# First z of a fused attention and expert kernel loaded in two parts, z copies issued by GpSimd, routing labels summed in two steps, last products reordered

## Chip, cores and metric

One Trainium2 chip, one core of it. The time is the device time of one execution in microseconds, lower is better. The engines are named as in the profile: PE (TensorE, products), PEld (its weight loads), DVE (VectorE), ACT (ScalarE), POOL (GpSimd), SP (SyncE, which here only issues DMAs). All data are float32 unless said otherwise.

## What is computed

Two blocks, one after the other: a gated attention unit over 8 batches of 2496 tokens, and a mixture of 8 experts to which each token goes by a hash of its id.

```python
batch, seq, d_model, d_qk = 8, 2496, 256, 64
def _attn_ref(u, v, z):
    scale = 1.0 / S
    scores = scale * np.matmul(z, z.transpose(0, 2, 1))
    attn = np.maximum(scores, 0.0) ** 2
    out = np.matmul(attn, v)
    return (u * out).astype(np.float32)

def _moe_ref(x, token_ids, w1, w2):          # x: (19968, 256), w1: (8, 256, 1024), w2: (8, 1024, 256)
    expert_idx = token_ids * np.int64(2654435761) % np.int64(8)
    for e in range(8):
        mask = expert_idx == e
        h = np.maximum(x[mask] @ w1[e], 0.0)
        out[mask] = h @ w2[e]
```

## The kernel before

**Attention.** A batch is cut into 5 groups of queries and 5 tiles of keys, so 25 steps, 200 in all; `pos` is the place of a step in its group (0 to 4). A step multiplies squared scores with v into an accumulator in PSUM (`attend`, L330), by a scheme with seven products for a 2x2 block product; the sums that it needs are made by DVE (`sums`, L279 to L282, and `add_v`, L218 to L221). Scores are symmetric: they are computed (`score`, L255 on PE, relu and square on ACT, L259 to L268, one square on DVE, L264) for key tiles not before the group, and else recalled from a mirrored copy in DRAM that earlier steps transposed (L295) and stored (L303, L307, on SP's queue). At `pos` 4 `join` (L341 to L349) adds the accumulators up, and the next group can only write a bank when `join` has read it. Scores are made two steps ahead (`AHEAD = 2`).

**z.** The scores need z transposed, `zT`, with the 64 values of a key on partitions 0 to 63 and the same again on partitions 64 to 127, for the second half of the keys. A batch has 78 blocks of 32 tokens, loaded in four pieces, `ZB = ((0, 16), (39, 55), (16, 39), (55, 78))`. `load_z` (L164) issues the loads of a piece, `turn_z` (L177) transposes it on DVE (L190, L192), up to 8 blocks an instruction. For batch 0, `twice(b)` holds: z is loaded to both halves of the partitions, so a piece has four loads instead of two, and at once before the first step. For each later batch, in the batch before, piece c is loaded at step 5 + 4c of it, turned at step 10 + 4c, and `copy_z` (L195) sends the lower half of the partitions to the upper by a DMA at step 11 + 4c; the fourth copy thus stands at step 23 of 25, and the scores of the next batch that read it are made from step 25 on. The z pool has two buffers, so the third piece waits for the first to be turned.

**Order.** The order of the work is written out by hand: each engine and each DMA queue takes its instructions in the order of the program. In one step that order is: sums and scores two steps ahead, storing mirrors, loading, turning and copying z of the next batch, `attend`, `join`, one mirror, loads of v, gating, one piece of the routing, sorting, up to two scatters of token numbers. SP's queue carries the stores of mirrors, the loads of z, the copies of zT, and the fetches (`x_row`, L376) and `u` loads (L227) for gating. POOL issues the scatters of gated rows (`sort`, L415, which wait for DVE), of token numbers (`enter`, L700), of zeros (L691), and the loads and stores of prepared weights (L722, L746).

**Routing.** `places` is a generator that computes from the token ids where each token goes. One piece of it, up to the next `yield`, is run at each step that is in `ROUTE`: not at `pos` 4, not in the first group of a batch. The piece with the labels (L542 to L545) falls on step 13, at `pos` 3, just ahead of a join.

**Experts.** Tokens of one expert stand in blocks of 512. In iteration `i` of the last loop, `up_big` of block i (seven products for each half of the hidden width, 14 parts, `U`), `down_big` or `down_last` of block i - 1 (seven parts, `D`) and `turn_x` of block i + 1 (`X`) are interleaved by a string of letters, `ORDER`; a letter runs its generator to the next `yield`. A lower case letter is the one small block.

**Start.** PE first multiplies an identity with itself (`warm`, L827), while z arrives.

## Time and profile before

| | us |
|---|---|
| three runs | 2425.05, 2430.60, 2436.82; median 2430.6 |
| the profiled execution | 2431.11 |
| its span, from first to last instruction | 2429.3 |
| PE busy in it | 2412.5 |
| attention, until the last scores are made | about 1426 |
| mean granted PE clock | 0.998 of full speed |

A line of the timeline gives start in us, length in us, engine, source line, operation, what is written and read, shapes, and how many instructions are merged; in square brackets, how long the engine had been idle and what ended that. An f32 product is two passes on PE, so a step's numbers of products stand doubled. The list of waits gives total us, times and the longest. A windows line gives start and end, length, then busy us and count of PE, PEld, DVE, ACT and POOL, then the granted PE clock, the share of the DMA engines' time and GB/s. A DMA's row is the issue of it; the landing is told apart.

### The profile page before, as it was taken

The page shows a single profiled execution, that of the slowest core. Times are in us where ns is not written, and L with a number is a line of the kernel's source. Part 1 is how long each engine was busy: PE and PEld are TensorE (multiplying, and loading weights), DVE is VectorE, ACT ScalarE, POOL GpSimd, SP SyncE. Part 2 cuts the span into 40 slices and gives each one's busy share as a digit, 9 for nine tenths or more (in the row PEclk, how much of TensorE's full clock was granted, in tenths as well). Part 3 has the DMA queues.
Part 4 walks back from the last instruction along what each step waited for, and adds up shares of the span by engine and source line. Part 5 has one row for each costly group of instructions (what it writes and reads, how often), then busy time and mean ns, then how long its engine had stood idle before and what let it go on. Part 6 is the DMA issues. An engine that isn't in the chain of part 4 may idle for free.

```text
span 2429.3 us, 32806 instructions
## 1 busy us (share of the span) xinstructions
PE 2412.5 (99%) x11247; PEld 2015.3 (83%) x11247; DVE 1817.1 (75%) x3808; ACT 725.7 (30%) x1210; POOL 694.6 (29%) x741
## 2 busy tenths in 40 slices
PE   9999999999999999999999999999999999999998
PEld 7787787787787787787787788989898988888887
DVE  7778788868868868868868667777777777777774
ACT  4324314314324314314324212222222222222221
POOL 0000101433433433433423112232323323232323
PEclk9999999999999999999999999999999999999999
DMA  7874667788788888788887776868777776867682
GB/s 152 219 197 111 161 181 217 230 278 254 238 261 252 229 269 253 229 277 245 247 241 226 210 228 213 267 219 261 239 234 259 230 256 217 259 223 252 226 270 101
DMA packets 423642, 554.61 MB, mean 228 GB/s; under 512 B 256129, under 2 KB 350161, under 8 KB 405041
## 3 DMA queue, kind: packets, MB, share of 16 engines
q1 hardware_dynamic: 350704, 327.02, 48.1%
q0 software_dynamic: 40320, 127.63, 15.0%
q10 hardware_dynamic: 32448, 97.86, 12.1%
q8 instruction: 88, 1.44, 0.2%
q14 instruction: 82, 0.66, 0.1%
HBM read 352.23 MB, written 196.06 MB: 226 GB/s over the span
## 4 chain that ended last, share of the span: by engine, by line
PE 97%; DMA 1%; DVE 1%; issue 1%; ACT 0%; POOL 0%; ACTq 0%; POOLq 0%; DVEq 0%
PE acc L330 49%; PE h_ps L1034 20%; PE o_ps L1072 19%; PE s_ps L255 9%; PE o_ps L1107 1%; DMA zT<-zT 1%; DMA a<-scores 0%; ACT a L259 0%; DMA zn<-in_z_dram 0%; POOL out_dram L976 0%; PE h_ps L1131 0%; DVE t L279 0%; DVE labels L543 0%; DVE t L281 0%; DVE t L280 0%
## 5 line engine op out<-in xcount | busy, mean ns | idle before, releaser
L259 ACT ACTIVATE a<-s_ps 128x512 f32<-128x512 f32 (+1 forms) x480 | 246.4, 600 | 728.3 <-PE s_ps L255 699.9
L330 PE MATMUL acc<-t,vc 128*128 128x256 f32 (+3 forms) x1600 | 402.3, 374 | 0.3 <-DVE t L279 0.3
L330 PEld LDWEIGHTS acc<-a,v_sb 128*128 128x128 f32 (+1 forms) x1600 | 295.2, 191 | 121.6 <-issue 46.5
L330 PE MATMUL acc<-a,v_sb 128*128 128x256 f32 (+3 forms) x1600 | 385.5, 384 | 1.1 <-DVE o L343 1.0
L415 POOL DMA_INDIRECT x_slots<-x_row,row x160 | 189.5, 1184 | 640.0 <-DVE x_row L393 534.2
L330 PE MATMUL acc<-t,v_sb 128*128 128x256 f32 (+3 forms) x1600 | 369.7, 373 | 0.0
L330 PEld LDWEIGHTS acc<-t,vc 128*128 128x128 f32 (+1 forms) x1600 | 303.3, 190 | 34.4 <-DVE t L279 0.7
L330 PEld LDWEIGHTS acc<-t,v_sb 128*128 128x128 f32 (+1 forms) x1600 | 303.4, 190 | 33.7
L1034 PE MATMUL h_ps<-xs,w 128*128 128x256 f32 (+1 forms) x1280 | 311.9, 376 | 0.0
L279 DVE TENSOR_TENSOR t<-a 128x512 f32<-128x512 f32 (+1 forms) x200 | 134.3, 672 | 209.1 <-ACT a L268 152.9
L1072 PE MATMUL o_ps<-h,w 128*128 128x256 f32 (+1 forms) x1216 | 283.9, 376 | 0.0
L1041 ACT ACTIVATE h<-h 128x512 f32<-128x512 f32 (+1 forms) x240 | 149.9, 625 | 410.6 <-DVE h L994 173.8
L1034 PEld LDWEIGHTS h_ps<-xs,w 128*128 128x128 f32 x1280 | 242.6, 190 | 28.7
L1072 PEld LDWEIGHTS o_ps<-h,w 128*128 128x128 f32 x1216 | 236.1, 195 | 23.7
L255 PE MATMUL s_ps<-zT 64*128 64x512 f32 (+1 forms) x960 | 240.9, 614 | 4.4 <-DMA zT<-zT 4.0
L1034 PE MATMUL h_ps<-xT,w 128*128 128x256 f32 (+1 forms) x960 | 231.1, 376 | 0.0
L295 DVE STREAM_TRANSPOSE mirror<-a 128x256 f32<-128x256 f32 x640 | 217.7, 406 | 0.0
L1072 PE MATMUL o_ps<-hs,w 128*128 128x256 f32 (+1 forms) x912 | 213.0, 376 | 0.6 <-DVE hs L1023 0.6
L976 POOL DMA_INDIRECT out_dram<-o_sb,idx x152 | 156.9, 1032 | 181.4 <-DMA o_sb<-o 146.7
L700 POOL DMA_INDIRECT slot_tokens<-token,addr x160 | 170.2, 1064 | 121.9 <-DVE addr L688 73.1
L330 PE MATMUL acc<-a,vc 128*128 128x256 f32 (+3 forms) x800 | 201.1, 373 | 0.0
L1034 PEld LDWEIGHTS h_ps<-xT,w 128*128 128x128 f32 x960 | 182.0, 190 | 22.2 <-DVE h L994 0.4
(193 smaller groups left out, 2634.5 us busy)
## 6 DMA issues: line engine op xcount, KB each, us to landing
w<-w_blocks SPq DMA_DIRECT2D x80, 1792.0 KB, 12.1
scores<-mirror SPq DMA_DIRECT2D x192, 256.0 KB, 4.8
a<-scores ACTq DMA_DIRECT2D x48, 1024.0 KB, 5.5
scores<-mirror SPq DMA_DIRECT2D x224, 128.0 KB, 3.1
a<-scores ACTq DMA_DIRECT2D x32, 896.0 KB, 5.5
w_blocks<-w POOLq DMA_DIRECT2D x16, 1792.0 KB, 8.8
u_sb<-in_u_dram SPq DMA_DIRECT2D x72, 256.0 KB, 4.9
xq<-x_slots SPq DMA_DIRECT2D x144, 128.0 KB, 12.6
```

What stands on the lines that cost most here:

```text
L255: nc.tensor.matmul(flat(ps)[:, 0:2 * w].rearrange("p (q c) -> p q c", q=2), tile_of_keys(b, h, s, j), q_h, start=True, stop=True)
L259: nc.scalar.activation(of[:, :, j, h].rearrange("p m q e -> p q m e"), flat(ps)[:, 0:2 * w].rearrange("p (q m e) -> p q m e", q=2, e=in_bl ...
L279: nc.vector.tensor_sub(t1, y12, y11)
L295: nc.vector.transpose(to, in_blocks(a, g)[:, :, j, h].rearrange("p i q (r t) -> p t i q r", t=2)[:, t])
L330: nc.tensor.matmul(acc[k][:, half, 0:w], x[0:n, j, :], y[0:n, j], start=(first and j == 0 and half == 0), stop=(last and j == 1), skip_gro ...
L415: st = nc.gpsimd.indirect_dma_start(out=x_dram[:, :], out_offset=bass.IndirectOffsetOnAxis(ap=row[0:m, c:c + 1], axis=0), in_=x_sb[0:m, q, ...
L700: st = nc.gpsimd.indirect_dma_start(out=slot_dram[:, None], out_offset=bass.IndirectOffsetOnAxis(ap=addr[0:n, to:to + 1], axis=0), in_=tok ...
L976: st = nc.gpsimd.indirect_dma_start(out=out[:], out_offset=bass.IndirectOffsetOnAxis(ap=idx[0:n, col:col + 1], axis=0), in_=o[0:n], in_off ...
L1034: nc.tensor.matmul(ps[:, r], w1[j][:, k, ts(f + r, P)], y, start=first and r == 0, stop=True, skip_group_check=True)
L1041: lambda o, i, k, ps=None: nc.scalar.activation(o, o if ps is None else ps, AF.Relu))
L1072: nc.tensor.matmul(ps, w2_block(w2[j], k)[:, f], x[:, f], start=first and f == 0, stop=f == FQ - 1, skip_group_check=True)
L1107: nc.tensor.matmul(ps[:, ts(t, P)], x[:, f, ts(t, P)], w2_block(w2[j], k)[:, f], start=first and t == 0 and f == 0, stop=f == FQ - 1, skip ...
```

## The change

Five edits.

1. The first two pieces of batch 0 (`ZB[0]` and `ZB[1]`, 16 blocks each) are loaded and turned in two parts of 8 blocks: first part of piece 0, first part of piece 1, turn both, then the second parts. So there are 16 loads instead of 8, alternating on SP's and ACT's queues as before, and the load of the first v tile is issued behind all of them, where it stood before the third piece's loads and still does.
2. The warm products are 9 instead of 12.
3. `copy_z` is issued by GpSimd instead of SP: 28 copies, 4 for each of batches 1 to 7. Their places in the program are as before, so on POOL each stands ahead of the scatters of its own step.
4. The labels (a reduction over 8 experts of 160 columns) are summed in two halves of 80 columns, with a `yield` between; the two instructions after it (`eid`) go with the second half. A `yield` inside a loop over two kinds of blocks, further on, is moved behind the loop, so two pieces become one. What lies between, masks, counting products, scan and rank sums, therefore runs one piece later; what comes after, as before.
5. The last iteration that has an `up_big` gets its own string: its last three letters are `UUD` instead of `UDU`, so the last down product of block NL - 2 stands behind the last up product.

```diff
@@ -103,6 +103,8 @@
     assert sorted(x for a, b in ZB for x in range(a, b)) == list(range(S // L))
     NZ = len(ZB)
 
+    FIRST = 8
+
     def pool(name, bufs, **kw):
         return ctx.enter_context(tc.tile_pool(name=name, bufs=bufs, **kw))
 
@@ -161,26 +163,27 @@
     uf, vf, zf = (x.rearrange("b s d -> (b s) d") for x in (u, v, z))
     zn, zT, v_sb, vc_sb, u_sb = {}, {}, {}, {}, {}
 
-    def load_z(b, c, engines=None):
-
-        j0, j1 = ZB[c]
+    def load_z(b, c, engines=None, at=slice(0, None)):
+
+        if not at.start:
+            zn[b, c] = zpool.tile([P, 24, L], F32, name="zn")
+        j0, j1 = range(*ZB[c])[at][0], range(*ZB[c])[at][-1] + 1
         n = j1 - j0
-        zn[b, c] = zpool.tile([P, 24, L], F32, name="zn")
         for i in range((P if twice(b) else K) // L):
             (nc.sync if engines is None else engines[i % len(engines)]).dma_start(
-                out=zn[b, c][ts(i, L), 0:n, :],
+                out=zn[b, c][ts(i, L), ds(at.start, n), :],
                 in_=zf[ds(b * S + j0 * L, n * L), ts(i % (K // L), L)].rearrange("(j r) k -> r j k", r=L))
 
     def twice(b):
         return b == 0
 
-    def turn_z(b, c):
-        j0, j1 = ZB[c]
-        if c == 0:
+    def turn_z(b, c, part=slice(0, None)):
+        j0 = ZB[c][0]
+        if c == 0 and not part.start:
             zT[b] = zpool.tile([P, S + L], F32, name="zT")
             nc.vector.memset(zT[b][:, S:S + L], 0.0)
         n = P if twice(b) else K
-        j = j0
+        j, j1 = range(*ZB[c])[part][0], range(*ZB[c])[part][-1] + 1
         while j < j1:
             g, first = divmod(j % (HS // L), 2 * QB)
             m = blocks(g)
@@ -194,7 +197,7 @@
 
     def copy_z(b, c):
         at = ds(ZB[c][0] * L, (ZB[c][1] - ZB[c][0]) * L)
-        nc.sync.dma_start(out=zT[b][K:P, at], in_=zT[b][0:K, at])
+        nc.gpsimd.dma_start(out=zT[b][K:P, at], in_=zT[b][0:K, at])
 
     def load_v(b, s, engine=None):
         engine = nc.sync if engine is None else engine
@@ -540,7 +543,10 @@
             nc.vector.tensor_tensor(mask[:], mask[:], label[:].unsqueeze(2).to_broadcast([P, E, C]), op=OP.mult)
             yield
             labels = route.tile([P, C], F32)
-            nc.vector.tensor_reduce(labels[:], mask[:].rearrange("p e c -> p c e"), axis=AX.X, op=OP.add)
+            for c in (slice(0, C // 2), slice(C // 2, C)):
+                nc.vector.tensor_reduce(labels[:, c], mask[:, :, c].rearrange("p e c -> p c e"), axis=AX.X, op=OP.add)
+                if not c.start:
+                    yield
             nc.vector.tensor_scalar(eid[:], eid[:], float(E), float(E), op0=OP.is_ge, op1=OP.mult)
             nc.vector.tensor_add(eid[:], eid[:], labels[:])
             yield
@@ -651,7 +657,7 @@
                 over = some[:, 0:nb * E].rearrange('p (j e) -> p j e', e=E)
                 nc.vector.tensor_tensor(over, *a_b(iota_b[:, 0:nb], end[0:1, :]), op=OP.is_ge)
                 nc.vector.tensor_reduce(of_block[:, b0:b0 + nb], over, axis=AX.X, op=OP.add)
-                yield
+            yield
             nc.vector.tensor_scalar(of_block[:], of_block[:], float(E - 1), None, op0=OP.min)
             over = some[:, 0:NB * E].rearrange('p (j e) -> p j e', e=E)
             nc.vector.tensor_tensor(over, *a_b(of_block[:], iota_e[0:1, :]), op=OP.is_equal)
@@ -823,15 +829,17 @@
 
 
     warm = mm_ps.tile([P, P], F32, name="warm", tag="mm")
-    for _ in range(12):
+    for _ in range(9):
         nc.tensor.matmul(warm[:], ident[:], ident[:], start=True, stop=True)
 
-    for c in range(NZ):
-        load_z(0, c, (nc.sync, nc.scalar) if c < 2 else None)
-        if c < 2:
-            turn_z(0, c)
-        if c == 1:
-            load_v(0, 0)
+    for part in (slice(0, FIRST), slice(FIRST, None)):
+        for c in range(2):
+            load_z(0, c, (nc.sync, nc.scalar), part)
+        for c in range(2):
+            turn_z(0, c, part)
+    load_v(0, 0)
+    for c in range(2, NZ):
+        load_z(0, c)
     for k in range(1, NT):
         load_v(0, k)
     AHEAD = 2
@@ -1151,7 +1159,8 @@
 
 
     ORDER = {"first": "UUUUGUUUGUUUUUUU", "second": "DUDUDUUDUUDUU" "XUxUDUXUDUUUU",
-             "other": "UuUDUuUXDUdUDU" "UDUDUxUDUXUDU", "end": "DDDDDDDd"}
+             "other": "UuUDUuUXDUdUDU" "UDUDUxUDUXUDU",
+             "last": "UuUDUuUXDUdUDU" "UDUDUxUDUXUUD", "end": "DDDDDDDd"}
 
 
     BIG, SMALL = [x for e in range(E) for x in (*range(e * FULL // E, (e + 1) * FULL // E), NL - 1 - e)], [[]] * (NL - 1) + [list(range(NL, NL + SMALLS))]
@@ -1173,7 +1182,7 @@
         if i == 0:
             x_sb = late.tile([P, 2, 2, D], F32, name="x_row")
             parts["G"] = gate_at_once(*done, x_sb, lambda: down_ps.tile([P, 2, D], F32, name="g_ps", tag="held", bufs=2))
-        for p in ORDER["first" if i == 0 else "second" if i == 1 else "end" if i == NL else "other"]:
+        for p in ORDER["first" if i == 0 else "second" if i == 1 else "end" if i == NL else "last" if i == NL - 1 else "other"]:
             next(parts.get(p, iter(())), None)
         for p in parts.values():
             assert next(p, None) is None and next(p, "end") == "end"
```

## The prediction

> **What bounds the kernel now.** I read the page's busy times first, then the list of what TensorE (PE) waited for, then the timeline around each of those waits, then the granted clock there. All lines here are of the kernel before.

> ```profile
> span 2429.3 us, 32806 instructions
> ...
> PE 2412.5 (99%) x11247; PEld 2015.3 (83%) x11247; DVE 1817.1 (75%) x3808; ACT 725.7 (30%) x1210; POOL 694.6 (29%) x741
> ```
> PE has no large hole: 16.8 us of the span without a product. An edit off PE can win only where PE waits or runs slowly. The waits (total us, times, longest):

> ```profile
> PE s_ps L255 <- DMA zT<-zT: 4.0, 2, 2.1
> ...
> PE acc L330 <- DVE o L343: 1.0, 1, 1.0
> ```
> The copies of zT that this change moves, and the join that the labels delay, head this short list. The first costs more than its 4.0 us. PE at the start of batch 4, then the same stretch of batch 6, which had no wait:

> ```profile
> 731.66 1.13 PE L255 MATMUL s_ps<-zT 64*128 64x512 f32 x2
> 734.72 2.27 PE L255 MATMUL s_ps<-zT 64*128 64x512 f32 x6 [1.93 <-DMA zT<-zT]
> 736.92 3.33 PE L330 MATMUL acc<-a,v_sb 128*128 128x256 f32 x8
> ...
> 744.50 0.71 PE L255 MATMUL s_ps<-zT 64*128 64x512 f32 x2
> ```
> ```profile
> 1099.83 2.00 PE L255 MATMUL s_ps<-zT 64*128 64x512 f32 x8
> 1101.75 1.99 PE L330 MATMUL acc<-a,v_sb 128*128 128x256 f32 x8
> ...
> 1107.99 2.00 PE L255 MATMUL s_ps<-zT 64*128 64x512 f32 x8
> ```
> From score to score batch 4 takes 744.50 - 731.66 = 12.84 us, batch 6 takes 1107.99 - 1099.83 = 8.16. So the stall cost 4.7, of which 1.93 is waiting. The rest is the eight products after it, 3.33 against 1.99, and their neighbours, and the clock column says why (the number before the DMA share and GB/s):

> ```profile
> 724.00:736.00 12.00, 10.07 (x45) 6.97 (x44) 10.54 (x25) 5.04 (x9) 0.00 (x0) 1.00 0.72 196
> 736.00:748.00 12.00, 12.00 (x45) 8.33 (x44) 10.30 (x28) 5.85 (x10) 7.18 (x7) 0.86 0.75 208
> ```
> 0.86 over 12 us is 3.4 us at half clock: an idle of 1.9 us was followed by slow products. Batch 5 has the same pair (score starts 915.67 and 928.66: 12.99, so 4.8 lost; clock 0.86 behind it). Together 9.5 us. The 1.0 us wait at the join was not followed by a lower clock (1.00).

> Why the copy was late in batch 4:

> ```profile
> 722.73 0.36 DVE L192 STREAM_TRANSPOSE zT<-zn 64x224 f32<-64x224 f32 x1
> ...
> 726.29 0.67 SPq L376 DMA_DIRECT2D x_row<-x  x1
> 727.05 0.96 SPq L227 DMA_DIRECT2D u_sb<-in_u_dram  x2
> 728.11 0.47 SPq L197 DMA_DIRECT2D zT<-zT  x1
> ```
> z was turned at 723.09. SP issued its copy at 728.11, behind a fetch (512 KB) and two u loads (256 KB each) that it had just sent on the same queue; it landed at about 734.6, 6.5 us later. The 28 copies land 2.2/3.4/6.8 us after issue (least, median, most).

> **The change, part by part.**

> *Copies on GpSimd.* The same 28 copies now follow POOL's order, not SP's. SP loses 28 issues of 0.48 us and the wait in front of each; nothing on PE's path waits for those issues but the copies themselves. On POOL the fourth copy of a batch stands ahead of the last scatter of token slots (L700) of the step before; what stands before it there ended before z was turned, in batches 3 to 7 (batch 4: 720.1 against 723.09; batch 5: 903.7 against 908.17). So it starts when z is turned, not 2.4 to 5.0 us after. From turned to the score that needs it there are 9.6, 8.6, 7.5, 9.3 and 11.1 us in batches 3 to 7; from SP's issue there were 6.9, 3.6, 3.6, 5.9 and 8.7. Batches 4 and 5 were those with 3.6. The trace has no such copy on POOL. Its issue is bounded by POOL's plain DMAs, 0.60 us (L746) and 0.87 us (L722); its landing from below by the fastest copy of SP, 2.2, from above by L746's 11.9 us for ten times the bytes. Nearest is SP's own copy: 3.4 median, and 2.2 to 4.5 where no 512 KB fetch is just ahead on its queue. I take 0.8 + 3.4 = 4.2 us, 3 us inside the tightest case, and 0.8 + 6.8 = 7.6 would miss batch 5 by 0.1. Both stalls and their slow clock go: -9.5 us. If all landings were as slow as L746's median of 8.8, batches 4 and 5 would stall by 0.2 and 1.3 us and about 1.5 would remain; -9.5 to 0 are the ends.

> What the copies delay on POOL: the eight scatters of zeros (L691), at 260.62 now, stand behind the second copy of batch 2, turned at 307.41; they take 28 us, so end near 336, and the scatter after them starts at 361.57 now. Then two L700 (361.57 to 364.9) stand before batch 2's fourth copy, which starts at 365.2 instead of 357.99: 7.8 us before 372.97, enough. An L700 at 1222.50 waits until 1242.60; the sort behind it runs at 1256.43 and the table is read at 1307. Each other delay is one issue. PE waits for none of these before the last stage.

> [...]

> *First z in parts.* PE's first score waits for both z blocks, whole:

> ```profile
> 0.74 1.99 SPq L170 DMA_DIRECT2D zn<-in_z_dram  x4
> 1.42 5.01 PE L827 MATMUL warm<-ident 128*128 128x128 f32 x24 [1.42 <-POOL ident masks.py:199]
> 6.33 0.77 DVE L190 STREAM_TRANSPOSE zT<-zn 128x256 f32<-128x256 f32 x2 [0.75 <-DMA zn<-in_z_dram]
> 6.83 4.41 PE L255 MATMUL s_ps<-zT 64*128 64x512 f32 x16 [0.40 <-DVE zT L190]
> ```
> Eight loads of 64 KB become sixteen of 32 KB; half the bytes come first. An issue costs 0.5 us at any of these sizes, so the last load of the first half is still the fourth on its queue, issued at 2.3. It lands no sooner than the first load did, 2.5 us after issue (4.8), and no later than now (6.3). With half the packets before it I take 5.2; a transpose of 0.42 and PE starts at 5.7 instead of 6.83: -1.1 us, ends 0 and -1.4 (nine warm products, 18 passes at 0.21, occupy PE until about 5.4). Behind it: the second half is issued by 4.9 and lands near 7.2, when PE has done the first score (5.7 + 1.9); ScalarE issues eight loads instead of four (until 4.9) and then loads its table (1.28), ready at 6.2 for a score at 6.9; v_sb is issued 1.3 us later and lands near 9.2 against 10.1 wanted; the third z block waits for its buffer until about 6.8 instead of 5.61, lands near 14.3 and is turned at about 14.2 to 16. All are covered, with 0 to 0.9 us to spare.

> The clock rose during the 24 warm passes: 0.21 us each at first, 0.11 at the end, the change at about 5.8, after 4.4 us of products. With nine, PE is busy up to that moment but for some 0.3 us. If the clock came 3.4 us later, scores at half speed would take back up to 1.7. [...]

> *Labels in two steps.* The join's first sum should have run before PE wanted the bank:

> ```profile
> 119.57 2.34 DVE L543 TENSOR_REDUCE labels<-mask 128x160 f32<-128x1280 bf16 x1
> ...
> 127.34 1.99 PE L330 MATMUL acc<-a,v_sb 128*128 128x256 f32 x8 [1.01 <-DVE o L343]
> ```
> Half the reduction (1.17 of 2.34) and L544, L545 (0.5 with their gaps) leave this step: DVE is free 1.7 us sooner, but the next square (L264) waits for ScalarE until 121.3 rather than running at 122.34. So the join moves by 1.0: -1.0 us, just the wait. All routing pieces up to the block table then run one step later: second half and L544/545 (1.7) where the mask (1.45) stood; the mask where DVE idled 1.66 soon after; the six count products and their ScalarE copies one step on; the scan (2.78) one set of sums later; the rank sum (1.49) before a wait of 0.42, with 3.17 idle next. Two loop pieces now share a step, so the rest of the routing stands where it did. If this cover were gone, the largest, the scan, would cost up to 2.8.

> *Last stage.* One down product (2 us on PE) changes place with the last up product. What can be won is the slow product at 2405.57: 2.06 against 1.95 to 1.98, so -0.1. The 0.58 wait behind it, for L988, remains. Two stores move 1 us later on an idle POOL.

> **Sum.** The profiled execution took 2431.1 us (span 2429.3 and 1.8 around it), 0.5 above the median of 2430.6. 2431.1 - 9.5 - 1.1 - 1.0 - 0.1 = **2419.4**, 0.46% below the median. About 0.5%, 12 us, is what a measurement of this kernel can tell from no change; the line is at 2418.4.

> **Rivals.** (A) The copies stay late: POOL's queue replaces SP's, and at least half of the 9.5 remains. For it: landings of 6.5 us in a stage whose DMA engines are 72 to 83% busy. Against it: starts 5.0 and 3.9 us earlier. Time: 2424 to 2429, say 2427; chance 0.15. (B) More is won: runs with a third stall, batch 6 having had only 5.9 us, make the median before dearer, and SP's queue, 28 waits shorter, brings loads sooner. A third stall is 4.7 more: 2415 against a like median; chance 0.2. (C) Slower: copies on POOL land over 11.1 us after z is turned, as only L746's slowest did (11.9). Then batches 3 to 7 all stall: 5 x 4.75 - 9.5 = +14.3 and, with the other gains of 2.2, 2443. It decides from a landing of about 10 us on; chance 0.05. (D) The split does nothing, because the second half's packets mix with the first's: 2420.5, within the forecast.

> **Chances.** The forecast (2416 to 2424, D included) 0.6. Faster by over 0.5%: B's 0.2 and 0.17 of the forecast's 0.6, 0.37. Slower: C, 0.05. Within: 0.58. Range for 8 in 10: 2413 to 2428, which holds the forecast and most of A and B.

> **What would show it.** Right: PE has no wait for zT, and no clock under 1.00 between the start and the end; the third score of batches 4 and 5 takes 8.16 us to the next; the first score starts near 5.7; no wait on L343's join. Wrong: a POOL copy that starts over 2 us after its transposes, or lands over 7 us after; a half clock in the first 12 us; a new wait of PE between 140 and 200 us.

## The result, and the profile after

The changed kernel takes 2422.01 us, median of 20 runs (2420.97 to 2423.88); the kernel before, 20 runs beside it, 2426.38 (2422.63 to 2436.82). The ratio is 0.9978, 95% interval 0.9972 to 0.9984: 4.4 us less at the medians, 0.2%, which is inside the 0.5% that the forecast called no change. The 2419.4 forecast is 2.6 us too low. The most telling figure is the spread: 14 us before, 3 us after.

The profiled executions are 2431.1 before and 2421.5 after, so this pair shows 9.6 us, twice the difference of the medians. The page of the changed kernel, its first lines:

```profile
span 2419.8 us, 32825 instructions
...
PE 2406.5 (99%) x11241; PEld 2011.5 (83%) x11241; DVE 1817.9 (75%) x3809; ACT 725.8 (30%) x1210; POOL 715.5 (30%) x769
```

What TensorE (PE) waited for in the changed kernel (total us, times, longest):

```profile
PE warm L833 <- POOL ident masks.py:199: 1.4, 1, 1.4
PE h_ps L1042 <- DVE h L1002: 0.9, 1, 0.9
PE s_ps L258 <- DVE zT L193: 0.8, 1, 0.8
PE o_ps L1080 <- DVE hs L1031: 0.6, 1, 0.6
```
The 4.0 us for copies of zT and the 1.0 us for the join are gone. The wait for zT that is left is for a transpose, at the very start, and it has grown from 0.4 to 0.8. The 0.9 for L1002 was not there before.

The third score of batch 4 and what follows, in PE's timeline after (start, duration, instruction), and the windows around it (length, busy time and count of PE, PEld, DVE, ACT and POOL, granted clock, DMA share, GB/s):

```profile
730.41 2.00 PE L258 MATMUL s_ps<-zT 64*128 64x512 f32 x8
732.34 1.99 PE L333 MATMUL acc<-a,v_sb 128*128 128x256 f32 x8
...
738.58 2.00 PE L258 MATMUL s_ps<-zT 64*128 64x512 f32 x8
```
```profile
732.00:744.00 12.00, 12.00 (x54) 9.06 (x53) 11.90 (x33) 7.73 (x12) 5.03 (x5) 1.00 0.62 154
```
738.58 - 730.41 = 8.17 instead of 12.84, and full clock. Batch 5 is the same (12.99 before, 8.17 after): 4.67 + 4.82 = 9.49 us, the forecast's 9.5. The copy, in POOL's timeline:

```profile
721.04 0.57 POOL L200 DMA_DIRECT2D zT<-zT  x1 [2.15 <-DVE zT L195]
```
z was turned at 720.7; the copy starts 0.3 us later, where SP's had started 5.0 later.

The start, in the timelines of VectorE and PE after:

```profile
3.71 0.45 DVE L193 STREAM_TRANSPOSE zT<-zn 128x256 f32<-128x256 f32 x1 [2.80 <-DMA zn<-in_z_dram]
4.71 0.45 DVE L193 STREAM_TRANSPOSE zT<-zn 128x256 f32<-128x256 f32 x1 [0.55 <-DMA zn<-in_z_dram]
5.95 0.45 DVE L193 STREAM_TRANSPOSE zT<-zn 128x256 f32<-128x256 f32 x1 [0.80 <-DMA zn<-in_z_dram]
```
```profile
1.43 4.21 PE L833 MATMUL warm<-ident 128*128 128x128 f32 x18 [1.43 <-POOL ident masks.py:199]
6.45 4.41 PE L258 MATMUL s_ps<-zT 64*128 64x512 f32 x16 [0.82 <-DVE zT L193]
```
Both first parts are turned at 5.16, where the forecast put the second at 5.6 (5.2 + 0.42). But the first score starts at 6.45, not 5.7: just when the third transpose ends (5.95 + 0.45). It is of the second part, columns that the first score does not read.

The labels in VectorE's timeline, and the join in PE's:

```profile
118.48 1.23 DVE L547 TENSOR_REDUCE labels<-mask 128x80 f32<-128x640 bf16 x1
120.96 1.23 DVE L267 TENSOR_TENSOR a<-a 128x1024 f32<-128x1024 f32 x1 [1.26 <-ACT a L262]
```
```profile
125.97 1.99 PE L333 MATMUL acc<-a,v_sb 128*128 128x256 f32 x8
```
Half the reduction, then a wait for ScalarE, as forecast (121.3 there), and no wait at the join. From the twelfth score of batch 0 to the first of batch 1 it is 73.93 us instead of 74.92: -0.99.

The new wait, in the expert stage:

```profile
1450.25 1.13 PE L1042 MATMUL h_ps<-xT,w 128*128 128x256 f32 x4 [0.87 <-DVE h L1002]
```
From the first up product to the last product is 967.20 us, 966.17 before: +1.03. The new order of the last stage, -0.12 by a run below, is in this figure. Behind the last product it is 8.51 us to the end of the span, 8.39 before: +0.12, which no term of the forecast had. All ten profiles with copies on GpSimd have 8.50 to 8.52 there and the four with copies on SP 8.38 to 8.40, so it goes with that edit; how it comes about is open.

So this pair is: copies -9.49, first score -0.38, labels -0.99, an interval of batch 3 +0.13, expert stage with the last stage +1.03, the end +0.12: -9.58, and the spans, 2429.3 and 2419.8, differ by as much. That leaves open why the medians differ by only 4.4, why the start won a third of its due, and whether the new wait belongs to the change.

### The profile page after: what moved, and what is told of

It is laid out like the page before. It is cut to its first block, busy times and chain, and to the rows that moved or that the text cites. A ratio compares the mean times of both kernels' runs of the same rounds, so it can differ in the third digit from the quotient of the medians.

```text
span 2419.8 us, 32825 instructions
## 1 busy us (share of the span) xinstructions
PE 2406.5 (99%) x11241; PEld 2011.5 (83%) x11241; DVE 1817.9 (75%) x3809; ACT 725.8 (30%) x1210; POOL 715.5 (30%) x769
## 4 chain that ended last, share of the span: by engine, by line
PE 98%; issue 1%; DVE 0%; DMA 0%; POOL 0%; ACT 0%; ACTq 0%; POOLq 0%; DVEq 0%
PE acc L333 50%; PE h_ps L1042 20%; PE o_ps L1080 19%; PE s_ps L258 9%; PE o_ps L1115 1%; DMA zn<-in_z_dram 0%; POOL out_dram L984 0%; PE h_ps L1139 0%; ACT a L262 0%; DVE hs L1031 0%; DVE hs L1030 0%; PE cnt_ps L566 0%; PE g_ps L405 0%; DVE h L1002 0%; DVE h L1001 0%
## 5 line engine op out<-in xcount | busy, mean ns | idle before, releaser
L1080 PEld LDWEIGHTS o_ps<-hs,w 128*128 128x128 f32 x912 | 174.9, 192 | 20.5 <-DVE hs L1031 1.0
```

Source lines behind the costliest of these rows:

```text
L1080: nc.tensor.matmul(ps, w2_block(w2[j], k)[:, f], x[:, f], start=first and f == 0, stop=f == FQ - 1, skip_group_check=True)
```

## The experiments

Twelve kernels ran, four each on three chips; those of one chip share the runs of the kernel before. Its medians were 2426.78 (27 runs, 2422.71 to 2433.77), 2425.18 (33 runs, 2421.36 to 2432.02) and 2424.68 (29 runs, 2420.99 to 2435.89). All of them compute the whole of the reference.

### First chip: where do the 9.5 us go?

*The kernel before once more* (no edit, one run, profiled).

> The kernel before, unchanged, profiled once more. Theory 1 (the cost of the late copies differs from execution to execution, and the profile that the forecast was made from was a dear one): batches 4 and 5 again show TensorE waiting for a copy of zT, but for another length in at least one of them, and a half clock of 3.4 us behind a wait only where the wait is long enough or lies right; the loss from score to score (12.84 - 8.16 = 4.7 and 12.99 - 8.16 = 4.8 us before) changes by more than 1 us in at least one, so that the two together cost between 2 and 8 us rather than 9.5. Rival (the stalls are fixed, and the gain of 9.5 was given back elsewhere in the kernel after): the same 1.9 and 2.1 us of wait, the same half clock, 9.5 again.

Measured: 2430.97. The half that mattered came true: batch 4 lost 0.12 us (from 4.7) and batch 5 lost 9.45 (from 4.8). But the two together cost 9.58, not 2 to 8: this execution lay as high as the first one. SP's and PE's timelines at batch 5 of this run, then its windows, cut at the steps of the clock:

```profile
906.21 0.50 SPq L376 DMA_DIRECT2D x_row<-x  x1
906.81 1.39 SPq L227 DMA_DIRECT2D u_sb<-in_u_dram  x2
908.30 0.47 SPq L197 DMA_DIRECT2D zT<-zT  x1
```
```profile
910.88 1.13 PE L255 MATMUL s_ps<-zT 64*128 64x512 f32 x2
915.93 3.75 PE L255 MATMUL s_ps<-zT 64*128 64x512 f32 x6 [3.92 <-DMA zT<-zT]
```
```profile
911.34:914.74 3.40, 0.67 (x2) 0.00 (x0) 3.26 (x9) 0.60 (x1) 0.00 (x0) 1.00 0.79 226
914.76:918.16 3.40, 2.23 (x5) 1.20 (x6) 3.40 (x11) 0.15 (x1) 0.00 (x0) 0.50 0.03 7
918.17:921.57 3.40, 3.40 (x7) 1.61 (x6) 2.63 (x8) 2.75 (x5) 1.24 (x1) 0.50 0.78 149
921.59:924.98 3.39, 3.39 (x10) 2.67 (x9) 2.57 (x5) 0.75 (x1) 2.91 (x3) 0.50 0.99 280
925.00:928.40 3.40, 3.40 (x17) 2.79 (x15) 3.40 (x11) 0.00 (x0) 2.61 (x3) 1.00 0.87 208
```
The queue is the same as before, a fetch of 512 KB (L376), two u loads, then the copy; PE got it 7.6 us after its issue (908.30 to 915.93). The wait of 3.92 us was followed by three stretches of 3.4 us at half clock. Beyond the wait the batch lost 5.5 us (9.45 - 3.92), in these stretches above all, in which PE was busy for 2.23, 3.40 and 3.39 us. A stall's price was not fixed here, in length or in what was lost beyond the wait: 4.7 us with a wait of 1.93 (batch 4 of the first profile), 9.45 with one of 3.92.

*Copies on GpSimd alone*, the one edit made to the kernel before:

```
-        nc.sync.dma_start(out=zT[b][K:P, at], in_=zT[b][0:K, at])
+        nc.gpsimd.dma_start(out=zT[b][K:P, at], in_=zT[b][0:K, at])
```

> The kernel before with one edit alone: the copies of z within zT are issued by GpSimd instead of SyncE. Theory 1 (the mean stall is worth 3 to 4 us and the other edits 1 to 2): ratio 0.9984, about 3 to 4 us below the kernel before, no wait of TensorE for zT by a DMA; the 1.0 us wait for the join at the end of the first row stays, and the first score starts at 6.8. Rival (the copies carry the whole gain or more, the other edits nothing): ratio 0.9978 or less. Rival (the copies bring nothing at the median, since their stall was only in some executions): ratio 0.9993 or more.

Measured: 2421.33 (2421.01 to 2421.61), ratio 0.9978 (0.9969 to 0.9987). The first rival: this edit alone carries the whole gain, 5.4 us here, and the spread falls from 11 us to 0.6. Even the best run of before, 2422.71, lies 1.1 over the highest of these. Less its 9.5 us of stalls, each profile of before gives nearly this kernel's time: 2431.1 - 9.5 = 2421.6, 2430.97 - 9.58 = 2421.4. The join's wait was not 1.0 but 0.27 us.

*The changed kernel with the copies back on SP* (the same line undone).

> The changed kernel with the copies of z back on SyncE; the first z in parts, the labels in two steps and the last stage stay changed. Theory 1: ratio 0.9992 to 0.9995 (0.4 from the start, 1.0 from the join, 0.1 at the end = 1.5 us, less some noise); TensorE waits for copies of zT again in batches 4 and 5, of 0 to 2.1 us each. Rival (these three edits carry the gain and the copies little): ratio 0.998. If the wait of 0.87 us for L1002's h in the expert stage (at 1450) is made by the copies on GpSimd, it is absent here; if it comes from the other edits or from chance, it may be here too.

Measured: 2422.56 (2420.19 to 2428.79), ratio 0.9989 (0.9978 to 1.0000), between theory and rival and not told from 1. Undoing the copies costs about 0.001 of the time, 2 to 3 us (0.9989 against the changed kernel's 0.9978 to 0.9982 here and below), less than the 5.4 that they won alone; the intervals leave room for both. By the plain medians of this chip (2422.56 against 2426.78) the other three edits alone would win 4.2; so the price of the copies in this company is known to a microsecond or two only, and why the stalls cost less here than in the kernel before is open. The long tail is back. The L1002 wait is absent. The profile had two short stalls, 0.27 and 0.95 us, and both cost just that (8.44 and 9.12 against 8.17 from score to score). They are between products that the list of waits takes as busy, and show in these distances only. A join in batch 3 waited 0.62 us more. It also showed the start going wrong. PE's timeline:

```profile
6.49 6.08 PE L258 MATMUL s_ps<-zT 64*128 64x512 f32 x16 [0.86 <-DVE zT L193]
12.51 1.99 PE L333 MATMUL acc<-a,v_sb 128*128 128x256 f32 x8
```
The same 16 products that took 4.41 us after took 6.08. The clock's first full grant in this trace is at 10.71, in that of after at 5.64; the first attend products start at 12.51 and 10.80, 1.7 apart. In these traces the clock's changes lie on a grid with steps of 3.41 us (more on them at the end); the step from 3.88 to 7.30 held the whole 0.86 us of idle here, and the rise came one step later. In the other thirteen profiles the step just ahead of the first rise held at most 0.44 us of idle.

*Second transposes behind the first score's products.* In the changed kernel:

```
-        for c in range(2):
-            turn_z(0, c, part)
+    for c in range(2):
+        turn_z(0, c, slice(0, FIRST))
...
+        between()
         for j, h, ps in made:
...
+    def rest_of_z():
+        for c in (1, 0):
+            turn_z(0, c, slice(FIRST, None))
```
(`between` is `rest_of_z` in the first score; v and the later z pieces are loaded after it.)

> The changed kernel with one thing moved: the transposes of the second halves of the first two z pieces are emitted behind the products of the first score, so that this score can no longer depend on them; the loads behind them move with them. Theory 2 (the start won 0.38 us instead of 1.1 because the first score waited for the third transpose, which it does not read, since dependencies are kept over the span of a strided access): TensorE's first score starts at 5.6 to 5.8 instead of 6.45, and the first attend product at about 10.0 to 10.2 instead of 10.80, 0.6 to 0.8 us less in all if the clock still rises at 5.6; ratio to the kernel before 0.0003 lower than the changed kernel's 0.9978. Rival (the start is bound by the landing of the z loads, not by the order of the transposes): first score again after 6.3. Rival (the clock rises one window of 3.4 us later because TensorE idles between the warm products and the score): first score at 5.7 but at half speed, and the first attend product no earlier than 10.8.

Measured: 2419.32 (2418.92 to 2420.71), ratio 0.9972 (0.9963 to 0.9981). The first score started at 5.56: its wait was the dependency on the third transpose, which is thereby shown. It did not wait for the fourth, which is behind its products now and writes beyond the last column that it reads (1504 to 1759; it reads up to 1503). The first attend product, at 10.76, was no earlier, since the clock rose at 6.85 in this run and the second score waited 0.67 us for its own transposes. The run was repeated below.

### Second chip: the start, and SP's order

*The changed kernel again.*

> The changed kernel, unchanged, beside the next three on one chip, and profiled a second time. Theory 2b (the nine warm products leave TensorE idle for 0.8 us before the first score, so that in most executions the clock rises one window of 3.4 us later, as it did with this start when the copies were on SyncE: 10.71 us instead of 5.64): the times spread over 2 us or more as before (2420.97 to 2423.88), and this profile shows the rise anywhere from 4.9 to 11 us. Theory 4 (the wait of 0.87 us for L1002's h in the expert stage is chance): it is absent in this profile. Rival to 4 (it belongs to the change): it is there again, 0.8 to 0.9 us at the same place.

Measured: 2421.52 (2420.20 to 2423.75), ratio 0.9982 (0.9973 to 0.9991); spread 3.6 us. The clock rose at 5.44. The wait for L1002 was 0.47: neither absent nor 0.8 to 0.9.

*First z whole again, 12 warm products.*

```
-    for _ in range(9):
+    for _ in range(12):
...
-    for part in (slice(0, FIRST), slice(FIRST, None)):
...
+    for c in range(NZ):
+        load_z(0, c, (nc.sync, nc.scalar) if c < 2 else None)
```

> The changed kernel with the first z loaded and turned whole again and 12 warm products instead of nine; copies, labels and last stage stay changed. Theory 2b (the start edit wins 0.4 us where the clock rises at 5.6 and loses up to 1.7 where it rises a window later): median 0.3 to 1.0 us BELOW the changed kernel's on the same chip, about 2421.0, and a spread under 1 us, like that of the copies alone (2421.01 to 2421.61). Rival (the start edit is worth its 0.4 to 0.6 us, as the first pair of profiles shows it): median 0.4 to 0.6 us ABOVE the changed kernel's.

Measured: 2421.49 (2420.51 to 2422.57), ratio 0.9981 (0.9972 to 0.9990). Neither: the median is that of the changed kernel to 0.03 us. The spread is 2.1, less than 3.6 but not under 1. No gain of the start edit is shown: the difference is -0.03 us, with an interval of -1.2 to +0.8 (of medians, drawn again and again from the eleven runs of each), which leaves room for the 0.4 of the profile.

*Twelve warm products, z in parts.*

```
-    for _ in range(9):
+    for _ in range(12):
```

> The changed kernel with 12 warm products instead of nine: TensorE has products until the transposed z is there, so no idle of 0.8 us lies ahead of the first score. Theory 2b: the clock rises at 5.0 to 8.3 in every execution, the spread falls below 1.5 us, the median lies 0.5 to 1.2 us below the changed kernel's on the same chip; in the profile no wait of TensorE for L193 over 0.3 us. Rival (the number of warm products is of no account, since TensorE has to wait for the third transpose until 6.4 anyway): the same median within 0.3 us and the same spread.

Measured: 2421.08 (2420.22 to 2422.37), ratio 0.9979 (0.9970 to 0.9988): 0.4 below the changed kernel, spread 2.2, wait for L193 0.37, clock up at 5.34. The direction is the theory's, both sizes miss its bounds, and the difference lies inside the intervals: not shown.

*The last fetch one step later, copies on SP*, in the kernel before:

```
-    FETCH = (1, 5, 8, 12, 15, 19, 22)
+    FETCH = (1, 5, 8, 12, 15, 19, 23)
```

> The kernel before, copies on SyncE, with one number changed: the last of the seven fetches of 512 KB in a batch is issued a step later, so behind the fourth copy of zT and not ahead of it on SyncE's queue. Theory 1 (what makes the copy late is what stands ahead of it on its queue): the long stalls go, ratio 0.9985 or less, landing of the fourth copies in batches 3 to 7 under 4 us after issue. Rival (the copy is late because SyncE reaches its issue late, behind waits of its own; only another engine cures that): ratio 0.9995 to 1.0005 and TensorE still waits for a copy of zT in one of the batches 3 to 7.

Measured: 2421.95 (2421.17 to 2423.27), ratio 0.9983 (0.9974 to 0.9992). SP's timeline in batch 4, and PE's at the start of the kernel with the window of that wait:

```profile
725.49 0.58 SPq L197 DMA_DIRECT2D zT<-zT  x1
726.26 0.98 SPq L380 DMA_DIRECT2D x_row<-x  x2
```
```profile
7.44 4.42 PE L255 MATMUL s_ps<-zT 64*128 64x512 f32 x16 [1.66 <-DVE zT L190]
```
```profile
4.41:7.80 3.39, 1.73 (x14) 1.49 (x15) 1.54 (x4) 0.00 (x0) 0.00 (x0) 1.00 1.11 223
```
The copy is ahead of the fetch now, and PE waits for none of the 28 copies, though SP still issues this one 2.3 us after z is turned. The two u loads moved with their fetch, so what changed is what stood ahead of the copy, and that did two things: it was issued 2.3 and 0.5 us after z was turned in batches 4 and 5, instead of 5.0 and 3.9, and no fetch stood just ahead of it any more. When it landed is not in this trace. The earlier issue alone (2.7 and 3.4 us) exceeds the stalls of 1.9 and 2.1, so the two are not told apart. What stood ahead on the queue made the copy late either way, and one digit in the kernel before wins about what the whole change does on the same chip, 0.9983 against 0.9982. It did not need another engine.

### Third chip: price of a stall, labels, and two repeats

*Transposes and copies one step later*, in the changed kernel:

```
-            for after, do in ((0, load_z), (5, turn_z), (6, copy_z)):
+            for after, do in ((0, load_z), (6, turn_z), (7, copy_z)):
```

> The changed kernel with the transposes and copies of the next z one loop step, some 8 us, later, so that the fourth copies (still on GpSimd) miss the score that reads them: many stalls in one profile, to price them. TensorE should wait 1 to 4 us in most of the batches 1 to 7. Theory 1b (the price of a stall is the wait plus what a half clock costs, and that half clock comes in stretches of 3.4 us, so 1.7 us each, or not at all): stalls with a wait under about 1.2 us cost the wait alone, longer ones the wait plus 1.7 us or a multiple of it, with less than 1.2 us left over, and half-clock stretches are multiples of 3.41 us. Rival (the price is proportional to the wait, 2.4 us for each us of wait as in batches 4 and 5 before): cost over wait between 2.2 and 2.6 throughout.

Measured: 2418.16, one run, the least of this study, and no stall at all: both expectations fell with their common premise. The fourth transposes of batch 4 ended 1.7 us later than after (722.4 for 720.7), not 8. What was won is elsewhere: in batches 0 to 6 the interval from the thirteenth to the fourteenth score, in which a row's join falls, took 14.23 us instead of 14.52. PE and VectorE in the changed kernel's profile on this chip:

```profile
842.67 1.90 PE L333 MATMUL acc<-t,v_sb 128*128 128x256 f32 x8
844.58 1.99 PE L333 MATMUL acc<-a,v_sb 128*128 128x256 f32 x8
846.41 1.03 PE L333 MATMUL acc<-t,vc 128*128 128x256 f32 x4
```
```profile
843.47 0.76 DVE L193 STREAM_TRANSPOSE zT<-zn 64x256 f32<-64x256 f32 x2
844.16 0.37 DVE L346 TENSOR_TENSOR o<-r,acc 128x256 f32<-128x256 f32 x1
```
and with the transposes a step later:

```profile
841.27 1.90 PE L333 MATMUL acc<-t,v_sb 128*128 128x256 f32 x8
843.00 1.89 PE L333 MATMUL acc<-a,v_sb 128*128 128x256 f32 x8
844.73 1.03 PE L333 MATMUL acc<-t,vc 128*128 128x256 f32 x4
```
```profile
842.07 0.41 DVE L346 TENSOR_TENSOR o<-r,acc 128x256 f32<-128x256 f32 x1
```
Two transposes (0.76) stood ahead of the join's first sum that reads the bank. The next row's product begins where that sum ends (844.16 + 0.37 = 844.53, start 844.58), 1.91 us behind the last group instead of 1.73, and its own eight take 1.83 instead of 1.73 to the next: 0.28 of the 0.29. Seven times 0.29 is 2.0 us, and with a first score 0.26 earlier in this run (6.37 for 6.63) 2.3; the spans differ by 2418.6 - 2416.4 = 2.2. No list of waits showed it. That the sum is what holds the product is read from these starts, not tried by itself.

*Labels in one step, last stage as before.*

```
-            for c in (slice(0, C // 2), slice(C // 2, C)):
-                nc.vector.tensor_reduce(labels[:, c], mask[:, :, c].rearrange("p e c -> p c e"), axis=AX.X, op=OP.add)
-                if not c.start:
-                    yield
+            nc.vector.tensor_reduce(labels[:], mask[:].rearrange("p e c -> p c e"), axis=AX.X, op=OP.add)
...
-            yield
+                yield
...
-              "last": "UuUDUuUXDUdUDU" "UDUDUxUDUXUUD", "end": "DDDDDDDd"}
+              "last": "UuUDUuUXDUdUDU" "UDUDUxUDUXUDU", "end": "DDDDDDDd"}
```

> The changed kernel with the labels summed in one step and the last stage's order put back; copies on GpSimd and the first z in parts stay. Theory 3 (the wait for the join is itself different from execution to execution, 0.27 to 1.01 us in the profiles so far, so the edit is worth about 0.5 us in the mean, not 1.0, and the last stage nothing): median 0.3 to 0.8 us above the changed kernel's on the same chip, and a wait of 0.2 to 1.1 us for the join's first sum in the profile. Rival (forecast as written, 1.0 + 0.1): 1.1 us above. Rival (what the labels win in the first batch is given back later): within 0.2 us of the changed kernel.

Measured: 2420.68 (2420.32 to 2422.84), ratio 0.9982 (0.9970 to 0.9994), 0.19 above the changed kernel: less than the theory's 0.3, within the rival's 0.2, and with an interval of -1.3 to +1.7, drawn as before, the medians decide nothing. The profiles do. PE's timeline at the join:

```profile
126.36 1.99 PE L333 MATMUL acc<-a,v_sb 128*128 128x256 f32 x8 [0.28 <-DVE o L346]
```
The edit has 0.28 to win here, not 1.01, and wins 0.26 in these profiles (59.73 us for 59.99 over the last three steps of batch 0). The wait was small, and what the edit won of it, it kept. In the five profiles with the labels in one step it was 1.01 and 0.72 (before, twice), 0.28, 0.28 and 0.27. The last stage's pair of groups takes 2.53 us (2394.87 to 2397.40) for 2.65 with the old order: -0.12.

*The changed kernel a third time.*

> The changed kernel, unchanged, as the mark for the two beside it on this chip, with a third profile of its start and its expert stage. Theory 2b: the clock's rise at 4.9 to 5.7, or after 9.8 at the cost of 1 to 1.7 us; the wait in the expert stage, 0.87 and 0.47 us in the two profiles so far, is again another size. Rival for that wait (it belongs to the change): 0.4 to 0.9 us again.

Measured: 2420.49 (2420.05 to 2422.00), ratio 0.9979 (0.9968 to 0.9991). Clock up at 5.25; no wait for L1002. Its sizes in three profiles of one kernel: 0.87, 0.47, 0. A wait at these up products was also in two others, 0.37 (12 warm products, for ScalarE) and 0.20 (the last fetch later, copies on SP), so it varies from execution to execution and does not need the copies on GpSimd; what makes it is open. The 12 times fall in two groups, seven at 2420.05 to 2420.52 and five at 2421.84 to 2422.00, and those with the labels undone likewise (eight up to 2420.76, four from 2422.20). The gap of 1.3 to 1.4 us is near the 1.7 that the late clock cost with this start. No profile of the changed kernel caught a late rise, so that this is the cause is argued, not shown. It can't be all of the spread, since the kernel with the first z whole and 12 warm products also spread over 2.1 us.

*Second transposes late, again.*

> The changed kernel with the second transposes behind the first score's products once more, now beside the changed kernel on one chip. Theory 2c (this start wins for two reasons: TensorE has no idle ahead of the first score, so the clock rises in the window it would have without any gap, by 8.3 us at the latest; and the first score comes 0.8 us earlier): median 1.0 to 2.2 us below the changed kernel's, the least of all versions; first score at 5.5 to 5.8. Rival (the 2 us that it lay below the copies alone on the other chip were the chips and chance, as its first attend product at 10.76 against 10.80 and 10.72 suggests): within 0.5 us of the changed kernel.

Measured: 2419.48 (2419.01 to 2420.50), ratio 0.9973 (0.9962 to 0.9984), 1.0 below the changed kernel on the same chip (interval -2.5 to -0.3) and with no gap over 0.42 us in its times. PE's timeline:

```profile
5.56 2.00 PE L258 MATMUL s_ps<-zT 64*128 64x512 f32 x8
8.22 2.00 PE L258 MATMUL s_ps<-zT 64*128 64x512 f32 x8 [0.66 <-DVE zT L193]
10.14 1.99 PE L334 MATMUL acc<-a,v_sb 128*128 128x256 f32 x8
```
With the clock up at 5.50 the first attend product comes at 10.14, 0.8 before the changed kernel's 10.97: what the forecast wanted of the split. This is the best version measured with an interval; it beats both kernels, by 0.27% and 0.04%. It was not run together with the later transposes.

## Why the prediction was right or wrong

| term | forecast | this pair of profiles | medians |
|---|---|---|---|
| copies | -9.5 | -9.49, and +0.12 at the end | -5.4 alone, 2 to 3 lost where undone |
| first z | -1.1 | -0.38 | not told from 0 |
| labels | -1.0 | -0.99 | with the last stage, not told from 0 |
| last stage | -0.1 | -0.12 (third chip; in the next line here) | |
| expert stage | none | +1.03 | 0 to +1 by execution |

*Copies: the mechanism right, the size wrong.* Start, cause and cure were as forecast. The issue took 0.58 us (0.52 to 0.74) for 0.8; where the traces have the landing of a batch's fourth copy, it was 2.5 to 6.6 us after its issue began, for 4.2, and no copy stalled PE in the ten profiles with copies on GpSimd. GpSimd's order did what was read from it: batch 2's third and fourth copies were issued late (340.5 and 363.5, the fourth due at 371.6), harmlessly. Two readings behind the 4.2 were off without harm: a landing is counted from the start of the issue, so "0.8 + 3.4" counts the issue twice; and "2.2 to 4.5 where no 512 KB fetch is just ahead" does not hold in the forecast's own trace, where the second and third copies of batch 1 landed 6.8 and 6.6 us after their issue with no fetch ahead. The failing step is the sum: "2431.1 - 9.5 - 1.1 - 1.0 - 0.1". It took one execution's stalls as the kernel's. The spread of the three runs shown, 2425.05 to 2436.82, was evidence that something in the kernel differs by execution, and the stalls were the largest thing in the profile that could. The median of those three, 2430.6, near which the profiled execution seemed to stand, became 2426.4 with 20. That both profiled executions of the kernel before held some 9.5 us of stalls is another draw. The forecast of 2419.4 came within 2.6 us of the measured time because it was taken from 2430.6, 4.2 above the median, with a gain of 11.2 instead of 4.4: two errors that mostly cancel, which is luck.

*First z: one step failed.* "A transpose of 0.42 and PE starts at 5.7": the data was there, half a microsecond sooner than forecast, but the score also waited for a transpose that it does not read. The score takes its queries in two stretches of zT's columns (0 to 255 and 1248 to 1503), and the third transpose writes between them, at 256 to 511. Moving that transpose, and the fourth, started the score at 5.56 both times. The doubt about the clock ("up to 1.7") had the size that a run then showed (12.51 for 10.80), and the sum should have carried it as a term rather than an aside.

*Labels and last stage: right in the pair*, by mechanism and by size. But the 1.0 was again one execution's wait: 0.27 and 0.28 in three others.

*Rivals.* No fourth copy, the one that is due soon, stayed late (A), and none stalled batches 3 to 7 (C). More was not won (B). D, the split does nothing, fits the medians, where no gain of it is shown, but for other reasons than it gave. No issue of a copy took GpSimd over 0.74 us in the ten profiles that have the copies there. Landings on GpSimd's queue were somewhat longer (medians of 3.6 to 5.5 us by profile, up to 10.0, for 3.4 to 4.0, up to 8.1, on SP's). The slow ones are the second copies of batches 3 to 7 (6.7 to 10.0 us), each issued 0.58 us behind a store of 1792 KB (`w_blocks`, L746) on GpSimd's own queue; where both landings are known, the copy lands 0.3 to 0.8 us behind that store. It is SP's case again, harmless because this copy has time. What lengthened the rest is not shown.

*The signs.* No wait for a copy, no clock under 1.00, 8.17 in both batches, no wait at the join: as named. The first score near 5.7 was the sign that failed, and it led to the cause. One sign of being wrong came up all the same, a copy that starts over 2 us after its transposes or lands over 7 us after: of the 28 copies in the changed kernel's profile seven start 7.0 to 10.5 us after their transposes and four 2.0, and the slow landings, where known, reach 10.0. TensorE waited for none, because only a batch's fourth copy is due soon; the sign should have been written for that one.

## What to carry to other kernels

Where the times of a kernel spread over more than the gain that is looked for (here 14 us, for 4.4), a stall seen in one profile is a draw from that spread: take its price from several profiles, or as the distance of the median from the least time. Before a late transfer is moved to another engine, look at what is ahead of it on its own queue, and on the one it would move to; one digit in the order of the fetches did as much here (0.9983 against 0.9982). And a tile written in parts did not free its first reader here while a later part lay within the reader's access, from its first column to its last: the first score started at 6.45 us, and at 5.56 with that part written behind it.

## What was not expected of the hardware

```profile
917.15:920.55 3.40, 1.67 (x6) 0.73 (x6) 3.33 (x12) 0.81 (x3) 0.00 (x0) 1.00 0.33 68
920.57:923.96 3.39, 3.39 (x8) 2.49 (x8) 3.35 (x12) 3.07 (x5) 0.65 (x1) 0.50 0.54 133
```
PE idle for 1.73 us of a step (51%; batch 4: 1.90) was followed by half a clock; idle for 1.66 us of one (49%, the wait of 1.66 shown above) was not, nor for 1.01. The border lies between, if it is one. At the ends of the traces, in the step in which PE stops, it is alike: 1.49 to 1.65 us of idle (four traces) was not followed by half a clock, 2.44 to 2.83 (four others) was. Why three half-clock stretches followed the wait of 3.92 us, the last one behind a step in which PE was busy throughout (918.17 to 921.57 above), stays open.
